# Decode attention over a long cache: one ring of aligned load slots on one queue, and V sums of 512 columns

## The chip, the cores and the metric

The kernel runs on one core of a Trainium2 chip. The metric is the device time of one execution in microseconds; a kernel's time is the median of its runs.

## The reference

One decode step of a transformer block for a batch of B = 2 with one new token each. All tensors are f32.

```python
xn = layernorm(x)                                  # x: (2, 1, 512)
q = (xn @ wq) as 32 heads of 128                   # wq: (512, 4096)
scores = q . k * 128 ** -0.5                       # k_cache: (2, 8, 32768, 128)
p = softmax(scores)                                # 4 query heads share one K and V head
o = p @ v                                          # v_cache: (2, 8, 32768, 128)
s = o @ wo                                         # wo: (4096, 512)
g = silu((relu(xn @ W_gate) * (xn @ W_up)) @ W_down)   # F = 1792
return x + s * g
```

The two caches are 268 MB each and every element is used once. The weights add 28 MB.

## The kernel before, in words

The caches are read in tiles of 4096 positions: 128 partitions x 32 rows x 128 floats, 2 MiB each, 16 KB a partition (NC = 4 pieces of NJ = 8 rows of DH = 128). There are 16 groups, one for each pair of batch and K/V head; a group has NU = 8 tiles of K and 8 of V. K tile and V tile t of the whole run are called k_t and v_t, t from 0 to 127.

One pass of the main loop, step s, works on K tile s and, OFF = 9 steps later, on V tile s - 9:

- k_transposes (L279): DVE transposes K tile s in two halves of 2048 columns (L284) into kts, of which there are two buffers.
- scores (L288): PE multiplies them with the queries, 16 matmuls of 256 columns in four column groups (L295). DVE takes the result out of PSUM, with the maximum of each row (L305).
- maximum (L309), once a group: PE and DVE bring the row maxima together and spread the negative maximum (nb, L329).
- weights (L332): ACT makes exponentials with their sums (L335), PE permutes them (pt, L339), DVE transposes them (pts, L343).
- values (L345): PE sums V over the positions of the tile. The four query heads of a group are the stationary operand, 128 x 4, and the moving operand is 128 x 128: 32 matmuls a tile (L351). They add up in one PSUM tile o_ps; row j goes to the column group j % 4.
- at a group's end: sums (L361) makes the reciprocal of the sum of the exponentials, take_o (L369) evicts o_ps, finish_group (L373) adds up the column groups with four small matmuls (L379) against the constant sel, and, every second group, multiplies with a tile of wo (L394) and adds to yacc, or, at the very end, forms the result (res).

Ahead of the loop stand the layer norm, the query projection (project_q, L184: 32 matmuls of 512 columns with the four tiles of wq, then copies and transposes) and, inside the first steps, the MLP (mlp_gu, mlp_down) with two tiles each of W_gate, W_up and W_down.

Loads. K tiles and wq share a pool of three 16 KB buffers (kpool), V tiles and the MLP weights another of three (vpool); wo has two buffers of its own. The function load (L116) gives the DMAs in turn to the queues of SP and ACT. The dictionary `ahead` says after which step of the loop a load is written: K tile t after step t - 2, V tile t after step t + 7. The very last V tile comes in three pieces (half, quarter, quarter).

The program is written in that order, but a scheduler then orders each engine's instructions, the DMA issues on SP and ACT among them; each engine runs its own list strictly in order. A DMA issue waits, on the engine that issues it, for the last reader of the buffer that it fills. Eight semaphores serve the DMAs in turn, so a DMA also waits until the one that last had its semaphore has landed.

Of the kernel before, what the change touches and what calls it, by code (L numbers as in the profile page):

```python
# [17 lines left out]
NBLK = NC * NJ  # L18
TK = P * NBLK
LAG = 1  # L20


@with_exitstack
def kernel(
# [37 lines left out]

    ident = const.tile([P, P], F32, name="ident")
    make_identity(nc, ident)
    sel = const.tile([P, REP], F32, name="sel")
    nc.vector.tensor_reduce(
        sel, ident.rearrange("p (g r) -> p r g", g=4)[:, :REP, :], axis=AX.X, op=ALU.add
    )
    same = const.tile([P, Q, REP], F32, name="same")
    nc.vector.tensor_reduce(  # L70
        same[:, 0, :],
# [41 lines left out]
    queues = [nc.sync, nc.scalar]  # L113
    issued = [0]

    def load(dst, src):  # L116
        queues[issued[0] % 2].dma_start(dst, src)
        issued[0] += 1

    def group(g):  # L120
        return g % B, g // B
# [10 lines left out]
            c += n  # L132

    def load_k(t):
        KT[t] = kpool.tile([P, NC, NJ, DH], F32, tag="k", name=f"k_{t}")
        load_tile(KT[t], kc, t, (NC,))

    def load_v(t):
        VT[t] = vpool.tile([P, NC, NJ, DH], F32, tag="v", name=f"v_{t}")
        load_tile(VT[t], vc, t, (NC,) if t < NG * NU - 1 else (2, 1, 1))  # L140

    def load_wo(hk):
        WO[hk] = work.tile([P, 2, 2, D], F32, tag="wo", name=f"wo_{hk}", bufs=2)
# [8 lines left out]
    wqt = {}  # L152

    def load_wq(k):
        wqt[k] = kpool.tile([P, 2, QW], F32, tag="k", name=f"wq_{k}")
# [6 lines left out]
    xc = const.tile([32, D], F32, name="xc")  # L162
    sq = const.tile([32, D], F32, name="sq")
# [20 lines left out]
    def project_q():  # L184
        pq = [ps_m.tile([P, 512], F32, tag="m", name=f"pq_{half}") for half in range(2)]
        for k in range(NKC):
            for half in range(2):
                for c in range(4):
                    nc.tensor.matmul(  # L189
                        pq[half][32 * c : 32 * c + 32, :],  # L190
                        xnt[:, k, :],
                        wqt[k][:, half, c * 512 : (c + 1) * 512],
                        start=(k == 0),
                        stop=(k == NKC - 1),
                    )
        for half in range(2):
            qs = work.tile([P, 512], F32, tag="row", name=f"qs_{half}")
            nc.vector.tensor_copy(qs, pq[half])
            for h in range(REP):
                rep = work.tile([P, 4, 4, Q], F32, tag="qrep", name=f"qrep_{half}_{h}")  # L200
# [16 lines left out]
    mlp = {}  # L217

    def load_gu(which, half):
        t = vpool.tile([P, 2, F], F32, tag="v", name=f"w{which}_{half}")  # L220
        w = wg if which == "g" else wu
        load(
            t.rearrange("p k f -> p (k f)"),
# [30 lines left out]
        mlp["ht"] = ht  # L254

    def load_d(half):
        t = vpool.tile([P, FH, D], F32, tag="v", name=f"wd_{half}")
# [87 lines left out]
    def values(t):  # L345
        g, u = divmod(t, NU)
        v, w = VT.pop(t), PT.pop(t)
        for c in range(NC):
            for j in range(NJ):
                a = j % 4  # L350
                nc.tensor.matmul(  # L351
                    o_ps[Q * a : Q * a + REP, :],
                    w[:, j, c * REP : (c + 1) * REP],
                    v[:, c, j, :],
                    start=(u == 0 and c == 0 and j < 4),
                    stop=(u == NU - 1 and c == NC - 1 and j >= 4),
                )

    OS, RL = {}, {}

# [6 lines left out]
        nc.vector.reciprocal(RL[g], pr[:, :1])  # L367

    def take_o(g):  # L369
        OS[g] = work.tile([P, P], F32, tag="os", name=f"os_{g}")  # L370
        nc.vector.tensor_scalar(OS[g], o_ps, RL.pop(g), None, op0=ALU.mult)  # L371

    def finish_group(g):  # L373
        b, hk = group(g)
        pr = ps_m.tile([P, 512], F32, tag="m", name=f"po_{g}")
        o2 = OS.pop(g).rearrange("p (q i) -> p i q", i=2)
        for i in range(2):
            for r in range(2):
                nc.tensor.matmul(  # L379
                    pr[64 * r : 64 * r + 64, i * REP : (i + 1) * REP],  # L380
                    o2[:, i, :],
                    sel,
                    start=True,
                    stop=True,
                )
# [31 lines left out]
        nc.vector.tensor_add(base, base, xy)  # L417

    for t in range(NK):
        at(ahead, t - 2, load_k, t)  # L420
        at(ahead, t + OFF - 2, load_v, t)
    for i in range(2):
        at(ahead, i - 2, load_gu, "g", i)
        at(ahead, i, load_gu, "u", i)
        at(ahead, i + 2, load_d, i)
# [8 lines left out]
    for s in sorted(k for k in ahead if k < 0):  # L434
        for f, a in ahead[s]:
            f(*a)
    project_q()

    for s in range(NK + OFF):
        v = s - OFF  # L440
# [52 lines left out]
```

## Time and profile before

| | |
|---|---|
| time, median of 3 runs | 1352.66 us (1352.29 to 1358.3) |
| the profiled execution: its own time / its span | 1354.88 us / 1352.5 us |
| PE busy (matmuls) | 856.8 us, 63% of the span, 13288 matmul instructions |
| DVE busy | 721.4 us, 53% |
| ACT busy | 73.5 us, 5% |
| read from HBM | 564.67 MB, 418 GB/s over the span |
| shares of the two load queues (q1, q10) | 49.8% and 49.0% of the 16 DMA engines' time |
| granted TensorE clock, mean | 0.804 |

How to read it. The span is the time from the first to the last instruction of the profiled execution; its own time is as the runs are timed, with what lies around the span. A row of a group of instructions reads: line, engine, operation, output<-inputs, partitions x elements, count | busy us, mean ns of one | idle time of the engine just before them and what ended it. A matmul in f32 is two instructions on PE, each with a weight load (PEld). In a row of waits stand who waited, for whom, us in total, how often, and the longest. A row of the timeline begins with the start and the length in us and merges neighbours of a kind. SPq and ACTq are the instruction queues of SP and ACT, from which DMAs are issued. GB/s is what all DMA engines moved, instruction fetches included.

### The profile page before, as it was taken

Reading aid. Unit: us, or ns where it says so; the run is one execution under the profiler, and the core shown is the slowest. Engines: PE = TensorE matmul, PEld = TensorE weight load, DVE = VectorE, ACT = ScalarE, POOL = GpSimd, SP = SyncE. Lnnn points to the kernel's source line nnn. Section 1 sums busy time; section 2 is a strip of 40 time slices with the busy share of each in tenths; the row PEclk is TensorE's granted clock in tenths of the full one; section 3 lists DMA queues with packets and bytes.
Section 4 is the critical chain, followed back from the end, with each engine's and each line's share of the span. In section 5 each row is a group of like instructions: output and inputs, shape, how many; then the busy total and the mean of one; then the engine's idle time right before and its main releaser. Section 6 shows DMA issues by size and latency. Waiting matters only on the chain.

```text
span 1352.5 us, 28835 instructions
## 1 busy us (share of the span) xinstructions
PE 856.8 (63%) x13288; PEld 502.2 (37%) x13288; DVE 721.4 (53%) x973; ACT 73.5 (5%) x261; POOL 1.3 (0%) x7
## 2 busy tenths in 40 slices
PE   2466667575765766557576656657666676665685
PEld 0123334334342433334333333433433343343454
DVE  2587655365554655454654655536555464635630
ACT  0002000000000100000000100000000010000010
POOL 0000000000000000000000000000000000000000
PEclk9678878778687878888878787878888788787887
DMA  9999999999999999999999999999999999999997
GB/s 398 428 378 414 421 430 429 429 404 429 430 429 430 427 430 429 429 430 429 429 430 430 418 428 430 428 431 415 427 430 429 429 406 430 430 429 407 390 393 292
DMA packets 40951, 566.52 MB, mean 419 GB/s; under 512 B 4462, under 2 KB 4478, under 8 KB 6784
## 3 DMA queue, kind: packets, MB, share of 16 engines
q1 hardware_dynamic: 20264, 284.70, 49.8%
q10 hardware_dynamic: 20536, 279.99, 49.0%
q8 instruction: 104, 1.70, 0.4%
q14 instruction: 15, 0.12, 0.0%
q0 software_dynamic: 32, 0.00, 0.0%
HBM read 564.67 MB, written 0.00 MB: 418 GB/s over the span
## 4 chain that ended last, share of the span: by engine, by line
issue 100%; POOLq 0%; POOL 0%
POOLq L488 0%; POOL ident masks.py:199 0%; POOL ident masks.py:197 0%; POOLq masks.py:199 0%; POOLq L475 0%
## 5 line engine op out<-in xcount | busy, mean ns | idle before, releaser
L284 DVE STREAM_TRANSPOSE kts<-k 128x2048 f32<-128x2048 f32 x256 | 585.2, 2295 | 337.5 <-DMA k<-in_A_k_cache_dram 337.4
L295 PE MATMUL s<-kts,qt 128*32 128x256 f32 x4096 | 418.3, 460 | 205.4 <-DVE kts L284 191.7
L351 PE MATMUL o_ps<-v,pts 128*4 128x128 f32 x8192 | 352.3, 327 | 243.5 <-DMA v<-in_A_v_cache_dram 218.5
L351 PEld LDWEIGHTS o_ps<-v,pts 128*4 128x4 f32 x8192 | 249.0, 100 | 347.6 <-issue 109.4
L295 PEld LDWEIGHTS s<-kts,qt 128*32 128x32 f32 x4096 | 178.5, 130 | 352.6 <-issue 188.9
L335 ACT ACTIVATE sc<-sc,nb 128x256 f32<-128x256 f32 x128 | 63.9, 499 | 1139.9 <-DVE nb L329 612.2
L305 DVE TENSOR_SCALAR_CACHE_REDUCE sc<-s 128x256 f32<-128x256 f32 x128 | 51.5, 402 | 137.0 <-PE s L295 136.6
L343 DVE STREAM_TRANSPOSE pts<-pt 128x256 f32<-128x256 f32 x128 | 55.1, 435 | 76.7 <-PE pt L339 67.5
L339 PE MATMUL pt<-sc,perm 128*128 128x256 f32 x256 | 95.6, 473 | 0.2 <-DVE l L363 0.2
L339 PEld LDWEIGHTS pt<-sc,perm 128*128 128x128 f32 x256 | 45.4, 213 | 52.5 <-issue 44.1
L335 ACT ACTIVATION_READ_ACCUMULATOR sc<-sc,nb 128x1 f32 x128 | 23.9, 187 | 0.0
L189 PE MATMUL pq<-wq,xnt 128*32 128x512 f32 x64 | 12.1, 908 | 9.4 <-DMA wq<-in_A_wq_dram 9.0
L211 DVE COPY qt<-pqt 32x16 f32<-32x16 f32 x64 | 8.6, 177 | 14.1 <-PE pqt L206 13.7
L394 PE MATMUL py<-wo,ot 128*32 128x128 f32 x256 | 15.8, 403 | 0.4 <-DVE ot L389 0.4
L371 DVE TENSOR_SCALAR os<-o_ps,rl 128x128 f32<-128x128 f32 x16 | 5.4, 338 | 19.0 <-PE o_ps L351 19.0
L233 PE MATMUL ps_u<-wu,xnp 128*32 128x448 f32 x32 | 6.5, 669 | 13.2 <-DMA wu<-in_B_W_up_dram 13.2
L394 PEld LDWEIGHTS py<-wo,ot 128*32 128x32 f32 x256 | 11.9, 162 | 4.4 <-issue 3.0
L389 DVE COPY ot<-po 64x4 f32<-64x4 f32 x32 | 5.1, 161 | 13.4 <-PE po L379 13.1
L329 DVE COPY nb<-pr 128x1 f32<-128x1 f32 x16 | 2.4, 148 | 18.1 <-PE pr L325 18.1
L177 PE MATMUL px<-ident,xc 32*128 32x32 f32 x4 | 0.9, 287 | 16.6 <-DVE xc L171 16.6
L305 DVE DVE_READ_ACCUMULATOR sc<-s 128x1 f32 x128 | 10.6, 83 | 0.0
L325 PEld LDWEIGHTS pr<-negone,mrow 1*128 1x128 f32 x32 | 6.5, 253 | 10.6 <-DVE os L371 7.3
(70 smaller groups left out, 111.1 us busy)
## 6 DMA issues: line engine op xcount, KB each, us to landing
k<-in_A_k_cache_dram SPq DMA_DIRECT2D x70, 2048.0 KB, 21.7
v<-in_A_v_cache_dram ACTq DMA_DIRECT2D x65, 2048.0 KB, 24.2
v<-in_A_v_cache_dram SPq DMA_DIRECT2D x62, 2048.0 KB, 22.1
k<-in_A_k_cache_dram ACTq DMA_DIRECT2D x58, 2048.0 KB, 23.9
wo<-in_A_wo_dram ACTq DMA_DIRECT2D x5, 1024.0 KB
wq<-in_A_wq_dram SPq DMA_DIRECT2D x2, 2048.0 KB, 12.7
wq<-in_A_wq_dram ACTq DMA_DIRECT2D x2, 2048.0 KB, 15.6
wg<-in_B_W_gate_dram ACTq DMA_DIRECT2D x2, 1792.0 KB, 12.5
```

Source lines behind the costliest of these rows:

```text
L189: nc.tensor.matmul(pq[half][32 * c : 32 * c + 32, :], xnt[:, k, :], wqt[k][:, half, c * 512 : (c + 1) * 512], start=(k == 0), stop=(k == N ...
L211: nc.vector.tensor_copy(qt[part, b, half * 4 : half * 4 + 4, :, kb * REP + h], src[:, :, :, b],)
L233: nc.tensor.matmul(ps[32 * c : 32 * c + 32, :FC], xnp[:, k, :], mlp[which, k][:, c * FC : (c + 1) * FC], start=(k == 0), stop=(k == NKC - 1),)
L284: nc.vector.transpose(KTS[t][:, i * half : (i + 1) * half], src[:, i * half : (i + 1) * half])
L295: nc.tensor.matmul(ps[Q * c : Q * c + Q, :], qt[:, b, hk, e, :], mov[:, e, c], start=(e == 0), stop=(e == 3),)
L305: nc.vector.tensor_scalar(ST[t], ps, SCALE, None, op0=ALU.mult, op1=ALU.max, accum_out=MX[g][:, u : u + 1])
L325: nc.tensor.matmul(pr[:, 256:257], mrow.rearrange("o c k h -> o (c k h)"), negone, start=True, stop=True)
L335: nc.scalar.activation(st, st, AF.Exp, bias=NBIAS[g], scale=1.0, accum_out=LS[g][:, u : u + 1])
L339: nc.tensor.matmul(ps, perm.rearrange("p k c h -> p (k c h)"), st, start=True, stop=True)
L343: nc.vector.transpose(PT[t].rearrange("p j m -> p (j m)"), ps)
L351: nc.tensor.matmul(o_ps[Q * a : Q * a + REP, :], w[:, j, c * REP : (c + 1) * REP], v[:, c, j, :], start=(u == 0 and c == 0 and j < 4), sto ...
L394: nc.tensor.matmul(py[32 * c : 32 * c + 32, :P], ot[:, k // 2, k % 2, :], WO[hk][:, k // 2, k % 2, c * P : (c + 1) * P], start=(k == 0), s ...
```

## The change

Four things change.

1. One pool, ring, with SLOTS = 8 slots of 16 KB takes the place of kpool, vpool and wo's two buffers. It is the first pool to be laid out, and each slot starts at a multiple of 512 bytes. K, V, wq, the MLP weights and wo all go through it. To make room, xp, xc, sq and the query copies (qrep) share one K^T buffer under the name boot.
2. All loads are issued by SP. Only x (boot, xy) and one piece of the result go through ACT.
3. Loads are written one step earlier (DEPTH = 3), V before K within a step, and each wo tile right behind the last V tile that is loaded for its head.
4. values sums with 8 matmuls a tile instead of 32: the stationary operand has the weights of all four pieces (128 x 16) and the moving operand one row j of all four (512 columns). o_ps grows to 128 x 512, of which only the blocks that belong together are used. take_o evicts 512 columns, and finish_group picks the blocks with 16 small matmuls instead of 4, against four versions of sel.

```diff
+LAST = (2, 1, 1)
+SLOTS = 8
+DEPTH = 3
+ALIGN = 512
...
+    ring = ctx.enter_context(tc.tile_pool(name="ring", bufs=SLOTS))
     const = ctx.enter_context(tc.tile_pool(name="const", bufs=1))
-    kpool = ctx.enter_context(tc.tile_pool(name="kpool", bufs=3))
-    vpool = ctx.enter_context(tc.tile_pool(name="vpool", bufs=3))
...
-    xp = const.tile([32, D], F32, name="xp")
+    boot = ktpool.tile([P, NBLK * DH], F32, tag="kt", name="boot")
+    xp, xc, sq = (boot[:32, i * D : (i + 1) * D] for i in range(3))
+    reps = [boot[:, (3 + i) * 512 : (4 + i) * 512] for i in range(2)]
...
-    o_ps = ps_p.tile([P, P], F32, name="o_ps", bufs=1)
+    o_ps = ps_p.tile([P, NC, DH], F32, name="o_ps", bufs=1)
...
-        queues[issued[0] % 2].dma_start(dst, src)
-        issued[0] += 1
+        nc.sync.dma_start(dst, src)
...
-        KT[t] = kpool.tile([P, NC, NJ, DH], F32, tag="k", name=f"k_{t}")
+        KT[t] = ring.tile([P, NC, NJ, DH], F32, tag="r", align_bytes=ALIGN, name=f"k_{t}")
...
-        for c in range(NC):
+        c = 0
+        for n in (NC,) if t < NK - 1 else LAST:
             for j in range(NJ):
-                a = j % 4
+                a = Q * (j % 4)
                 nc.tensor.matmul(
-                    o_ps[Q * a : Q * a + REP, :],
-                    w[:, j, c * REP : (c + 1) * REP],
-                    v[:, c, j, :],
+                    o_ps[a : a + n * REP, :n, :],
+                    w[:, j, c * REP : (c + n) * REP],
+                    v[:, c : c + n, j, :],
...
+            c += n
...
-                nc.tensor.matmul(
-                    pr[64 * r : 64 * r + 64, i * REP : (i + 1) * REP],
-                    o2[:, i, :],
-                    sel,
-                    start=True,
-                    stop=True,
-                )
+                for c in range(NC):
+                    nc.tensor.matmul(
+                        pr[64 * r : 64 * r + 64, i * REP : (i + 1) * REP],
+                        o2[:, c, i, :],
+                        sel[:, c, :],
+                        start=(c == 0),
+                        stop=(c == NC - 1),
+                    )
...
-        at(ahead, t - 2, load_k, t)
-        at(ahead, t + OFF - 2, load_v, t)
+        at(ahead, t - DEPTH, load_k, t)
+        at(ahead, t + OFF - DEPTH, load_v, t)
...
-        at(ahead, (hk * B + B - 1) * NU + OFF + NU // 2 - 1, load_wo, hk)
+        at(ahead, (hk * B + B) * NU - 1 + OFF - DEPTH, load_wo, hk)
```

How the change moves instructions shows at three places. The names carry numbers: k_28 is K tile 28, sc_19 the scores of K tile 19, pt_8 and pts_8 the permuted and the transposed weights of tile 8, s_16 the score sums of K tile 16; the last number is that of the buffer.

The first place is the issue of loads in the third group. ACT before, whose list holds every second load, here the K tiles:

```order
L117 DMA k_28_1908<-in_A_k_cache_dram 128x4096
L335 ACTIVATE sc_19_1376,ls_2_1709<-sc_19_1376,nb_2_1707 128x256
L117 DMA k_29_1971<-in_A_k_cache_dram 128x4096
L335 ACTIVATE sc_20_1439,ls_2_1709<-sc_20_1439,nb_2_1707 128x256
L117 DMA k_30_2034<-in_A_k_cache_dram 128x4096
L335 ACTIVATE sc_21_1504,ls_2_1709<-sc_21_1504,nb_2_1707 128x256
```

SP in the changed kernel, which has them all:

```order
L123 DMA v_14_1196<-in_A_v_cache_dram 128x4096
L123 DMA k_23_1198<-in_A_k_cache_dram 128x4096
L123 DMA v_15_1235<-in_A_v_cache_dram 128x4096
L123 DMA k_24_1237<-in_A_k_cache_dram 128x4096
L123 DMA wo_0_1239<-in_A_wo_dram 128x2x1024
L123 DMA v_16_1276<-in_A_v_cache_dram 128x4096
L123 DMA k_25_1278<-in_A_k_cache_dram 128x4096
```

On ACT the K loads stood between exponentials of the group at hand; on SP there are loads alone, V and K in turn, in the order in which they are used.

The second place is a group's boundary on PE, from the last V tile of the first group on (pr_1 belongs to the maximum of the second group, pl_0 to the sum of the first, po to finish_group). Before:

```order
L351 MATMUL o_ps_123<-v_7_1070,pts_7_1099 4x128 x15
L295 MATMUL s_16_1140<-kts_16_1137,qt_114 32x256 x14
L313 MATMUL pr_1_1162<-ident_82,m_1_1160 1x128
L365 MATMUL pl_0_1181<-l_0_1179,same_89 128x1
L295 MATMUL s_17_1233<-kts_17_1230,qt_114 32x256 x5
L325 MATMUL pr_1_1162<-negone_101,mrow_99 128x1
L295 MATMUL s_17_1233<-kts_17_1230,qt_114 32x256 x4
L379 MATMUL po_0_1219<-sel_87,os_0_1217 64x4 x4
```

And in the changed kernel:

```order
L316 MATMUL pr_1_988<-ident_79,m_1_986 1x128
L371 MATMUL pl_0_1007<-l_0_1005,same_89 128x1
L355 MATMUL o_ps_123<-v_7_881,pts_7_949 16x512 x4
L328 MATMUL pr_1_988<-negone_101,mrow_99 128x1
L355 MATMUL o_ps_123<-v_7_881,pts_7_949 16x512 x3
L342 MATMUL pt_8_1001<-sc_8_665,perm_96 128x256
L386 MATMUL po_0_1021<-sel_84,os_0_1019 64x4 x16
L342 MATMUL pt_9_1067<-sc_9_710,perm_96 128x256
L342 MATMUL pt_10_1106<-sc_10_749,perm_96 128x256
L342 MATMUL pt_11_1145<-sc_11_788,perm_96 128x256
L342 MATMUL pt_12_1184<-sc_12_827,perm_96 128x256
L298 MATMUL s_16_966<-kts_16_963,qt_114 32x256 x16
```

Before, the scores of K tiles 16 and 17 stood ahead of and between the steps of the maximum; now the scores of K tile 16 come behind the whole maximum and five tiles of weights. DVE's list has its two transposes of K tile 16 behind pts_10 in the same way.

The third place is the end of the loads. SP before (ACT had v_120, v_122, v_124, two pieces of v_127 and, ahead of these, wo_7):

```order
L117 DMA v_119_8686<-in_A_v_cache_dram 128x4096
L117 DMA v_121_8815<-in_A_v_cache_dram 128x4096
L117 DMA v_123_8893<-in_A_v_cache_dram 128x4096
L117 DMA v_125_8971<-in_A_v_cache_dram 128x4096
L117 DMA v_126_9012<-in_A_v_cache_dram 128x4096
L117 DMA v_127_9051<-in_A_v_cache_dram 128x1024
```

SP in the changed kernel:

```order
L123 DMA v_125_6152<-in_A_v_cache_dram 128x4096
L123 DMA v_126_6167<-in_A_v_cache_dram 128x4096
L123 DMA v_127_6182<-in_A_v_cache_dram 128x2048
L123 DMA v_127_6182<-in_A_v_cache_dram 128x1024 x2
L123 DMA wo_7_6186<-in_A_wo_dram 128x2x1024
```

The last tile of wo, before issued ahead of V tile 120, is now the last load of all.

More of the change, by code (lines that the diff above doesn't have):

```diff
@@ L64 @@
     make_identity(nc, ident)
-    sel = const.tile([P, REP], F32, name="sel")
-    nc.vector.tensor_reduce(
-        sel, ident.rearrange("p (g r) -> p r g", g=4)[:, :REP, :], axis=AX.X, op=ALU.add
-    )
+    sel = const.tile([P, NC, REP], F32, name="sel")
+    for c in range(NC):
+        nc.vector.tensor_reduce(
+            sel[:, c, :],
+            ident.rearrange("p (g r) -> p r g", g=4)[:, c * REP : (c + 1) * REP, :],
+            axis=AX.X,
+            op=ALU.add,
+        )
     same = const.tile([P, Q, REP], F32, name="same")
@@ L134, in load_k @@
     def load_k(t):
-        KT[t] = kpool.tile([P, NC, NJ, DH], F32, tag="k", name=f"k_{t}")
+        KT[t] = ring.tile([P, NC, NJ, DH], F32, tag="r", align_bytes=ALIGN, name=f"k_{t}")
         load_tile(KT[t], kc, t, (NC,))
     def load_v(t):
-        VT[t] = vpool.tile([P, NC, NJ, DH], F32, tag="v", name=f"v_{t}")
-        load_tile(VT[t], vc, t, (NC,) if t < NG * NU - 1 else (2, 1, 1))
+        VT[t] = ring.tile([P, NC, NJ, DH], F32, tag="r", align_bytes=ALIGN, name=f"v_{t}")
+        load_tile(VT[t], vc, t, (NC,) if t < NG * NU - 1 else LAST)
     def load_wo(hk):
-        WO[hk] = work.tile([P, 2, 2, D], F32, tag="wo", name=f"wo_{hk}", bufs=2)
+        WO[hk] = ring.tile([P, 2, 2, D], F32, tag="r", align_bytes=ALIGN, name=f"wo_{hk}")
         r = REP * DH
@@ L154, in load_wq @@
     def load_wq(k):
-        wqt[k] = kpool.tile([P, 2, QW], F32, tag="k", name=f"wq_{k}")
+        wqt[k] = ring.tile([P, 2, QW], F32, tag="r", align_bytes=ALIGN, name=f"wq_{k}")
         load(wqt[k].rearrange("p h n -> p (h n)"), wq[k * P : (k + 1) * P, :])
@@ L161 @@
     st = const.tile([32, 8], F32, name="st")
-    xc = const.tile([32, D], F32, name="xc")
-    sq = const.tile([32, D], F32, name="sq")
     nc.vector.reduce_sum(st[:, 0:1], xp, axis=AX.X)
@@ L199, in project_q @@
             for h in range(REP):
-                rep = work.tile([P, 4, 4, Q], F32, tag="qrep", name=f"qrep_{half}_{h}")
+                rep = reps[h % 2].rearrange("p (e k l) -> p e k l", e=4, k=4)
                 qh = qs[:, h * DH : (h + 1) * DH].rearrange("p (e l) -> p e l", l=Q)
@@ L219, in load_gu @@
     def load_gu(which, half):
-        t = vpool.tile([P, 2, F], F32, tag="v", name=f"w{which}_{half}")
+        t = ring.tile([P, 2, F], F32, tag="r", align_bytes=ALIGN, name=f"w{which}_{half}")
         w = wg if which == "g" else wu
@@ L256, in load_d @@
     def load_d(half):
-        t = vpool.tile([P, FH, D], F32, tag="v", name=f"wd_{half}")
+        t = ring.tile([P, FH, D], F32, tag="r", align_bytes=ALIGN, name=f"wd_{half}")
         load(
@@ L347, in values @@
         v, w = VT.pop(t), PT.pop(t)
-        for c in range(NC):
+        c = 0
+        for n in (NC,) if t < NK - 1 else LAST:
             for j in range(NJ):
-                a = j % 4
+                a = Q * (j % 4)
                 nc.tensor.matmul(
-                    o_ps[Q * a : Q * a + REP, :],
-                    w[:, j, c * REP : (c + 1) * REP],
-                    v[:, c, j, :],
-                    start=(u == 0 and c == 0 and j < 4),
-                    stop=(u == NU - 1 and c == NC - 1 and j >= 4),
+                    o_ps[a : a + n * REP, :n, :],
+                    w[:, j, c * REP : (c + n) * REP],
+                    v[:, c : c + n, j, :],
+                    start=(u == 0 and j < 4),
+                    stop=(u == NU - 1 and c + n == NC and j >= NJ - 4),
+                    skip_group_check=True,
                 )
+            c += n
     OS, RL = {}, {}
@@ L369, in take_o @@
     def take_o(g):
-        OS[g] = work.tile([P, P], F32, tag="os", name=f"os_{g}")
+        OS[g] = work.tile([P, NC, DH], F32, tag="os", name=f"os_{g}")
         nc.vector.tensor_scalar(OS[g], o_ps, RL.pop(g), None, op0=ALU.mult)
@@ L375, in finish_group @@
         pr = ps_m.tile([P, 512], F32, tag="m", name=f"po_{g}")
-        o2 = OS.pop(g).rearrange("p (q i) -> p i q", i=2)
+        o2 = OS.pop(g).rearrange("p c (q i) -> p c i q", i=2)
         for i in range(2):
             for r in range(2):
-                nc.tensor.matmul(
-                    pr[64 * r : 64 * r + 64, i * REP : (i + 1) * REP],
-                    o2[:, i, :],
-                    sel,
-                    start=True,
-                    stop=True,
-                )
+                for c in range(NC):
+                    nc.tensor.matmul(
+                        pr[64 * r : 64 * r + 64, i * REP : (i + 1) * REP],
+                        o2[:, c, i, :],
+                        sel[:, c, :],
+                        start=(c == 0),
+                        stop=(c == NC - 1),
+                    )
         o3 = pr[:, : 2 * REP].rearrange("p (i c r) -> p c i r", i=2, r=2)
@@ L432 @@
     at(extra, NK + OFF - 2, make_base)
-    for s in sorted(k for k in ahead if k < 0):
+    for f, a in ahead[-DEPTH] + ahead[1 - DEPTH]:
+        f(*a)
+    project_q()
+    for s in range(2 - DEPTH, 0):
         for f, a in ahead[s]:
             f(*a)
-    project_q()
     for s in range(NK + OFF):
```

8 lines of the change are left out of this document (3 added, 5 removed).

## The prediction

> **What bounds the kernel now.** I read the page first, for the loads:
>
> ```profile
> span 1352.5 us, 28835 instructions
> DMA  9999999999999999999999999999999999999997
> GB/s 398 428 378 414 421 430 429 429 404 429 430 429 430 427 430 429 429 430 429 429 430 430 418 428 430 428 431 415 427 430 429 429 406 430 430 429 407 390 393 292
> DMA packets 40951, 566.52 MB, mean 419 GB/s; under 512 B 4462, under 2 KB 4478, under 8 KB 6784
> q8 instruction: 104, 1.70, 0.4%
> ```
>
> Most slices stand at 427 to 431 GB/s; about ten fall to 292 to 421. The DMA digit is 9 in nearly all of them, so it does not tell good slices from bad; GB/s does. Next I asked for stretches, cut where the rate changes; the last three columns are the granted clock, the DMA share and GB/s:
>
> ```profile
> core 0: us, PE busy (x) PEld busy (x) DVE busy (x) ACT busy (x) POOL busy (x), PEclk, DMA share, GB/s
> 0.00:50.00 50.00, 21.76 (x134) 6.62 (x135) 19.25 (x64) 1.58 (x2) 0.70 (x6) 0.86 0.97 408
> 50.00:120.00 70.00, 36.87 (x437) 17.74 (x435) 48.91 (x102) 2.84 (x3) 0.00 (x0) 0.78 0.98 396
> 120.00:250.00 130.00, 86.35 (x1359) 51.70 (x1363) 76.57 (x93) 8.09 (x32) 0.00 (x0) 0.82 1.01 427
> 250.00:310.00 60.00, 38.41 (x577) 21.37 (x568) 34.11 (x39) 3.88 (x14) 0.00 (x0) 0.75 0.99 414
> 310.00:760.00 450.00, 288.35 (x4540) 170.77 (x4540) 240.94 (x289) 22.57 (x82) 0.00 (x0) 0.79 1.01 429
> 760.00:1200.00 440.00, 285.37 (x4513) 170.25 (x4513) 241.15 (x293) 26.03 (x96) 0.00 (x0) 0.82 1.00 426
> 1200.00:1265.00 65.00, 42.89 (x625) 25.78 (x629) 34.45 (x47) 3.28 (x12) 0.00 (x0) 0.76 0.96 398
> 1265.00:1305.00 40.00, 26.13 (x486) 16.42 (x479) 20.40 (x30) 1.09 (x4) 0.00 (x0) 0.90 1.01 428
> 1305.00:1346.00 41.00, 28.76 (x594) 20.32 (x593) 4.35 (x14) 4.15 (x16) 0.00 (x0) 0.77 0.89 354
> 1346.00:1352.50 6.50, 1.88 (x56) 1.23 (x44) 1.26 (x5) 0.00 (x0) 0.65 (x1) 0.93 0.00 1
> ```
>
> For 450 us on end (310 to 760) the loads run at 429 GB/s while PE is busy 64% and DVE 54%. I take 429 as the rate of a fed DMA. All bytes at that rate are 566.52 MB / 429 GB/s = 1320.6 us, so 31.9 us of the span are holes. By stretch, each us x (1 - GB/s / 429): 2.4 at the start, then 5.4, 0.6, 2.1, 0, 3.1, 4.7, 0.1 and 7.2, and 6.5 after the last load; 32.1 together. The kernel is bound by its loads, and the middle holes are 23.2 us.
>
> Why are there holes? The waits of SP's own queue:
>
> ```profile
> SPq L117 <- PE o_ps L351: 370.4, 64, 29.4
> SPq L117 <- DMA v<-in_A_v_cache_dram: 260.2, 48, 17.4
> SPq L117 <- DMA k<-in_A_k_cache_dram: 224.1, 56, 11.2
> SPq L117 <- DVE kts L284: 192.1, 30, 24.3
> ```
>
> A load waits until PE or DVE has freed one of only three buffers of its kind, and then often longer, for an earlier DMA. The two kinds do not share buffers: at the end only V is left and three of the six 16 KB buffers serve it, and that is the worst stretch (354). In between, ACT's half of the loads stands among its exponentials, which wait for a group's maximum.
>
> **The change part by part.** *The ring.* Eight slots serve loads strictly in order of use, so load n+8 waits for the user of load n, and for nothing else that is late. A 2 MiB load takes 2.097 MB / 429 = 4.9 us. When load n lands, seven others are issued or issuable, 34 us of DMA work. The queue runs dry only if a slot is still held about 34 us after its landing, less the time that an idle queue needs to begin, bounded above by a 1 KB transfer's 1.6 us from issue to landing; so 32 us decide. What holds a slot:
>
> ```profile
> out_dram<-res POOLq DMA_DIRECT2D x1, 1.0 KB, 1.6
> L284 DVE STREAM_TRANSPOSE kts<-k 128x2048 f32<-128x2048 f32 x256 | 585.2, 2295 | 337.5 <-DMA k<-in_A_k_cache_dram 337.4
> L295 PE MATMUL s<-kts,qt 128*32 128x256 f32 x4096 | 418.3, 460 | 205.4 <-DVE kts L284 191.7
> L351 PE MATMUL o_ps<-v,pts 128*4 128x128 f32 x8192 | 352.3, 327 | 243.5 <-DMA v<-in_A_v_cache_dram 218.5
> 1291.83 2.30 DVE L284 STREAM_TRANSPOSE kts<-k 128x2048 f32<-128x2048 f32 x1
> 1308.63 0.45 DVE L343 STREAM_TRANSPOSE pts<-pt 128x256 f32<-128x256 f32 x1 [2.38 <-PE pt L339]
> ```
>
> A K tile is held for two transposes, 2 x 2.295 = 4.6 us; a V tile for 352.3 / 128 = 2.8 us. The exception is a group boundary, where the new order puts the next group's first scores (PE) and transposes (DVE) behind the whole chain maximum, exponential, first weights. That chain, from the last K tiles (1291.83) to the first weights (1309.08), lasts 17.3 us, a wait of PE for a V tile included. Add the tile's own 4.6 and it is 21.9, below 32. Behind the waiting SP instruction stand all further loads; none is late as long as this holds. DVE catches up afterwards: 54% busy. So I take nothing for it (bounds 0, and 16 boundaries of a few us: below).
>
> At the start the first eight loads (four of wq, two of K, two of the gate: 6 x 2.097 + 2 x 1.835 = 16.25 MB) keep the DMA busy until about 2.4 + 37.9 = 40 us, and the ninth needs only the projection from the first wq, which before began at 18 us. The thirteenth (about 59 us) needs K tile 0, transposed before by 45.2 us:
>
> ```profile
> 18.00 6.49 PE L189 MATMUL pq<-wq,xnt 128*32 128x512 f32 x32 [0.39 <-DVE xnt L181]
> 42.85 2.30 DVE L284 STREAM_TRANSPOSE kts<-k 128x2048 f32<-128x2048 f32 x1
> ```
>
> The initial 2.4 us stay. The boot buffer, shared by the query work and a K^T tile, delays only K tile 1, whose slot the fifteenth load asks for near 68 us (28.05 MB before it). x now leaves ACT's queue ahead of the weights, so the layer norm comes earlier, hidden under wq. All 23.2 us of middle holes go.
>
> *One queue.* Does one queue reach 429? In 286 to 292 us the loads came from ACT's queue (q10) alone:
>
> ```profile
> DMA packets 175, 2.57 MB, mean 429 GB/s; under 512 B 18, under 2 KB 18, under 8 KB 18
> q10 hardware_dynamic: 174, 2.57, 100.1%
> ```
>
> 2.57 MB is more than one tile, so a change of load inside one queue is in it: cost 0. The Trainium skill's "DMA: Bandwidth & Descriptors", section "Anatomy of one DMA", gives each DMA a fixed 2.0 us beside its bytes; if one queue exposed that at each of 276 loads, an estimate from that page would be 550 us more. The stretch just quoted shows none of it.
>
> *Alignment.* The six big buffers before begin at multiples of 512 as built; only the wo tiles did not. Taken as 0.
>
> *Sums over V.* 32 matmuls a tile become 8 of 512 columns. The same shape in the query projection, 16 instructions (a matmul counts as two here):
>
> ```profile
> 26.01 1.92 PE L189 MATMUL pq<-wq,xnt 128*32 128x512 f32 x16 [1.52 <-DMA wq<-in_A_wq_dram]
> 35.42 3.64 PE L189 MATMUL pq<-wq,xnt 128*32 128x512 f32 x16 [7.49 <-DMA wq<-in_A_wq_dram]
> ```
>
> So 1.9 to 3.6 us a tile instead of 2.8: between 0.9 saved and 0.8 lost, all beside loads (9.8 us a step, of which PE is busy 64%). Time from this alone: 0; without that cover the 0.8 would cost 128 x 0.8 = 102 us. The wider eviction and finish of a group hide likewise. It does shorten the program: 8192 - 2048 matmuls, each with its weight load, leave 12288 fewer instructions; the fourfold sums in a group's finish add 16 x 24 x 2 = 768; 17.3 thousand remain. Instruction fetches (1.70 MB on the same engines) fall by 40%, 0.68 MB, 1.6 us.
>
> *The tail.*
>
> ```profile
> 1344.24 2.15 PE L351 MATMUL o_ps<-v,pts 128*4 128x128 f32 x64 [0.57 <-DMA v<-in_A_v_cache_dram]
> 1346.87 0.41 PE L379 MATMUL po<-sel,os 128*64 128x4 f32 x8 [0.49 <-DVE os L371]
> 1347.72 1.08 PE L394 MATMUL py<-wo,ot 128*32 128x128 f32 x32 [0.44 <-DVE ot L389]
> L198 DVE COPY qs<-pq 128x512 f32<-128x512 f32 x2 | 1.2, 664 | 0.0
> ```
>
> Before, V's last matmuls end at 1346.39; the last quarter of 64 takes about 0.6, so the loads end near 1345.8, and py starts 1.9 later. Now wo's last tile (1.05 MB, 2.4 us) lands behind V. After V: 0.6 of matmuls, the old 1.3 to py, 0.3 more for evicting 512 columns (664 ns for that shape) and about 1.0 for 32 small matmuls instead of 8: 3.2, or 0.8 after wo. So 1.1 us are gained (bounds 2 gained, 1 lost). On the clock: the slow row above (3.64) came after a wait of 7.49. The Trainium skill's "TensorE: Matmul & The Clock Gate", section "Part 1: The HAM clock gate", says the array falls to half clock after an idle window of about 3.4 us; PE idles more between V tiles now, and by that rule the tail's 2 us of PE work could double, making the sum 1 to 2 us longer. The pair of rows agrees with it.
>
> *Sum.* 1352.5 - 23.2 - 1.6 - 1.1 = 1326.6 of span. That execution took 1354.88 in all, 2.4 outside its span; the median of the runs, 1352.66, is 0.2 above the span, so a median of **1327 us**, 1.9% faster.
>
> **The rivals.**
> (a) *Part of the holes is not waiting.* The shares fall less than the rates: against 1.01, the deficits are 0.03 x 70, 0.02 x 60, 0.01 x 440, 0.05 x 65 and 0.12 x 41 = 15.9 us of the 23.2. The other 7.3 are packets that run long; if these have another cause than refilling an empty queue they stay: 1334. Against: they are long only near idle stretches.
> (b) *The holes move to the boundaries,* about as large as before: 1346 to 1359. For: the new order at a boundary. Against: the 21.9 us.
> (c) *Slower: one late slot stops everything.* A single in-order queue has no second one to go on with. It decides when a slot is held over 32 us: if the boundary chain doubled, 2 x 17.3 + 4.6 = 39.2, 7.2 us would be lost 16 times, 115 us: about 1442; at 35 us it is 3 x 16, about 1375. Nothing in the trace is that long.
> (d) *Slower: every load exposes its start and end* on one queue; with 1.6 us (the 1 KB row) x 276 = 440 us: 1767. The 429 row speaks against it.
> (e) *Only alignment or a deeper queue lifts the rate itself* over 429: at 432, 0.7% or 9 us less, 1318. Against: buffers already aligned, 429 to 431 wherever fed.
>
> **How the numbers follow.** The forecast has 0.80; its own range is 1321 to 1333 (rate 428 to 430, 3 us each way, and the tail's bounds). (a) 0.09, (b) 0.03, (c) 0.04, (d) 0.01, (e) 0.03. The range 1319 to 1340 holds the forecast, (a) and the edge of (e). What a measurement can tell from no change is 0.5%, 6.8 us: faster means under 1345.9. Forecast, (a) and (e) all lie there, less a little of (a) that I shift to the middle: faster 0.90, same 0.05, slower 0.05.
>
> **What would show it.** Right: GB/s at 427 to 431 in every slice but the first and last, all bytes on one queue, SP waiting for PE and DVE alone in the middle, DVE still waiting for K; instructions near 17.3 thousand; wo landing last, py within a us of it. Wrong: slices under 425 at a period of one group, some 80 us (b, c); a rate under 425 with the queue never empty (d); PE's V row over 5 us a tile.

## The result, and the profile after

The changed kernel takes 1333.68 us (median of 4 runs, 1332.56 to 1335.89), the kernel before, run beside it, 1354.36 us (1352.29 to 1358.3). The ratio is 0.9846, 95% interval 0.9832 to 0.986: 20.7 us faster. The forecast was 1327 us, 25.7 us under the 1352.66 us that it started from. So the time is 6.7 us longer than the sum said, and the gain 5 us smaller. The direction, the range and most of the mechanism held.

The page of the changed kernel, for the loads (GB/s in 40 equal slices, then the queues):

```profile
span 1334.0 us, 17338 instructions
GB/s 397 429 431 429 431 430 430 429 431 431 429 430 431 430 430 430 429 430 432 430 430 422 428 430 431 429 416 429 429 430 430 415 430 429 431 431 414 430 430 283
DMA packets 40907, 565.79 MB, mean 424 GB/s; under 512 B 4462, under 2 KB 4478, under 8 KB 6784
q1 hardware_dynamic: 40776, 564.68, 99.4%
q8 instruction: 60, 0.98, 0.3%
```

The early dips of before are gone: one queue, q1, moves 429 to 431 GB/s slice after slice. Four slices in the second half fall to 414 to 422, at every second group's boundary; x (1 - GB/s / 430) x 33.35 us they make 4.1 us. The last slice, 283, is much like before's, 292. What SP waits for (us in total, times, longest):

```profile
SPq L123 <- PE o_ps L355: 568.6, 120, 10.4
SPq L123 <- DVE kts L287: 448.3, 112, 10.1
SPq L123 <- PE py L401: 60.1, 7, 8.6
```

But for some 9 us on loads of wq and K, SP no longer waits for an earlier DMA, only for the work that frees slots, and there never longer than 10.4 us. The groups of instructions show something that was not forecast:

```profile
L287 DVE STREAM_TRANSPOSE kts<-k 128x2048 f32<-128x2048 f32 x256 | 572.7, 2275 | 0.0
L298 PE MATMUL s<-kts,qt 128*32 128x256 f32 x4096 | 466.7, 522 | 388.9 <-DVE kts L287 373.7 <-DVE l L369 9.4 <-DVE qt L214 3.2
L308 DVE TENSOR_SCALAR_CACHE_REDUCE sc<-s 128x256 f32<-128x256 f32 x128 | 54.3, 425 | 375.5 <-PE s L298 375.5
L355 PE MATMUL o_ps<-v,pts 128*16 128x512 f32 (+2 forms) x2080 | 360.2, 675 | 0.0
```

DVE, 55% busy, does not wait for K at all: it transposes, waits for PE's scores (375.5 us in all), transposes again, and PE waits for the transposes (373.7 us). A step is a trip DVE, PE, DVE in series, nearly as long as its loads, so landed tiles pile up in the ring. The V sums, in the last row, gain nothing on PE: 360.2 us over 128 tiles are 2.8 us a tile, as before. In this execution the last V sums come in one lump and late:

```profile
1317.72 8.80 PE L355 MATMUL o_ps<-v,pts 128*16 128x512 f32 x112
1327.40 1.46 PE L386 MATMUL po<-sel,os 128*64 128x4 f32 x32 [0.87 <-DVE os L377]
1329.29 1.08 PE L401 MATMUL py<-wo,ot 128*32 128x128 f32 x32 [0.43 <-DVE ot L396]
```

So the first theory was: the lag costs the 4 us of holes and some 3 us of a late end, and that is the miss. The experiments contradict it.

### The profile page after: what moved, and what is told of

It reads as the page before. It is cut to its first block, busy times and chain, and to the rows that moved or that the text cites. A ratio compares the mean times of both kernels' runs of the same rounds, so it can differ in the third digit from the quotient of the medians.

```text
span 1334.0 us, 17338 instructions
## 1 busy us (share of the span) xinstructions
PE 881.1 (66%) x7560; PEld 345.6 (26%) x7560; DVE 736.5 (55%) x976; ACT 69.1 (5%) x261; POOL 1.3 (0%) x7
## 4 chain that ended last, share of the span: by engine, by line
issue 100%; POOLq 0%; POOL 0%
POOLq L497 0%; POOL ident masks.py:199 0%; POOL ident masks.py:197 0%; POOLq masks.py:199 0%; POOLq L484 0%
## 5 line engine op out<-in xcount | busy, mean ns | idle before, releaser
L298 PE MATMUL s<-kts,qt 128*32 128x256 f32 x4096 | 466.7, 522 | 388.9 <-DVE kts L287 373.7
L287 DVE STREAM_TRANSPOSE kts<-k 128x2048 f32<-128x2048 f32 x256 | 572.7, 2275 | 0.0
L355 PE MATMUL o_ps<-v,pts 128*16 128x512 f32 (+2 forms) x2080 | 360.2, 675 | 0.0
L308 DVE TENSOR_SCALAR_CACHE_REDUCE sc<-s 128x256 f32<-128x256 f32 x128 | 54.3, 425 | 375.5 <-PE s L298 375.5
L355 PEld LDWEIGHTS o_ps<-v,pts 128*16 128x16 f32 (+2 forms) x2080 | 96.2, 116 | 141.6 <-issue 130.1
L342 PE MATMUL pt<-sc,perm 128*128 128x256 f32 x256 | 85.3, 439 | 33.4 <-DVE pts L346 32.2
L342 PEld LDWEIGHTS pt<-sc,perm 128*128 128x128 f32 x256 | 42.5, 198 | 99.7 <-issue 73.0
L386 PE MATMUL po<-sel,os 128*64 128x4 f32 x512 | 23.4, 204 | 3.9 <-DVE os L377 3.9
L386 PEld LDWEIGHTS po<-sel,os 128*64 128x64 f32 x512 | 22.0, 138 | 10.2 <-DVE os L377 10.2
L377 DVE TENSOR_SCALAR os<-o_ps,rl 128x512 f32<-128x512 f32 x16 | 12.0, 750 | 17.3 <-PE o_ps L355 17.3
L401 PE MATMUL py<-wo,ot 128*32 128x128 f32 x256 | 19.2, 403 | 0.4 <-DVE ot L396 0.4
L308 DVE DVE_READ_ACCUMULATOR sc<-s 128x1 f32 x128 | 10.7, 83 | 0.0
```

What stands on the lines that cost most here:

```text
L287: nc.vector.transpose(KTS[t][:, i * half : (i + 1) * half], src[:, i * half : (i + 1) * half])
L298: nc.tensor.matmul(ps[Q * c : Q * c + Q, :], qt[:, b, hk, e, :], mov[:, e, c], start=(e == 0), stop=(e == 3),)
L308: nc.vector.tensor_scalar(ST[t], ps, SCALE, None, op0=ALU.mult, op1=ALU.max, accum_out=MX[g][:, u : u + 1])
L342: nc.tensor.matmul(ps, perm.rearrange("p k c h -> p (k c h)"), st, start=True, stop=True)
L355: nc.tensor.matmul(o_ps[a : a + n * REP, :n, :], w[:, j, c * REP : (c + n) * REP], v[:, c : c + n, j, :], start=(u == 0 and j < 4), stop=( ...
L386: nc.tensor.matmul(pr[64 * r : 64 * r + 64, i * REP : (i + 1) * REP], o2[:, c, i, :], sel[:, c, :], start=(c == 0), stop=(c == NC - 1),)
```

## The experiments

Each time stands beside runs of the kernel before on the same chip (medians 1354.5 to 1355.0); ratios are to those.

### Transposes ahead of the scores' eviction

```diff
-        if s < NK:
-            k_transposes(s)
-            scores(s)
+        if s == 0:
+            k_transposes(0)
+        if s + 1 < NK:
+            k_transposes(s + 1)
+        if s < NK:
+            with tc.issue_after(TR[min(s + 1, NK - 1)].ins):
+                scores(s)
```

TR holds the second transpose of each tile; issue_after keeps the eviction on DVE behind it. Below, this kernel is called the one with the transposes ahead.

> The transposes of K tile s+1 are put ahead of the eviction of the scores of tile s on DVE, so that DVE transposes while PE multiplies; nothing else changes. Theory 1 (a step of the changed kernel is a serial trip DVE, PE, DVE about as long as its loads, so the ring slowly fills with landed tiles): the waits of DVE for PE's scores (375 us) fall below 100 us, DVE waits for K again, the four holes (4.4 us) go and the V sums end about 3 us earlier: 1325 to 1328 us instead of 1333.7. Theory 2 (the wo tiles, which hold ring slots until py, make the holes): the four holes stay where they are, at every second group's boundary, 1332 to 1334. Theory 3 (the wider eviction and the 16 small matmuls at a group's end make the boundary too long): the holes stay too, 1332 to 1334.

Measured: 1332.57 us (1332.06 to 1332.91), ratio 0.9838 (0.9825 to 0.9851). GB/s, the instruction fetches, and two groups of DVE:

```profile
GB/s 396 431 430 430 430 431 430 430 429 432 429 431 430 430 430 431 428 431 431 431 429 431 430 429 430 431 430 429 430 431 430 430 431 429 429 430 430 431 430 274
q8 instruction: 59, 0.97, 0.3%
```

```profile
L288 DVE STREAM_TRANSPOSE kts<-k 128x2048 f32<-128x2048 f32 x256 | 573.4, 2278 | 88.7 <-DMA k<-in_A_k_cache_dram 88.5
L309 DVE TENSOR_SCALAR_CACHE_REDUCE sc<-s 128x256 f32<-128x256 f32 x128 | 49.3, 385 | 3.0 <-PE s L299 3.0
```

Every sign of theory 1 came true: the wait for scores falls from 375.5 to 3.0 us, DVE waits for K again, no slice between the first and the last is under 428. Only the time did not follow: 1 us instead of 6 to 9. Where it goes shows at the end. Stretches of the last 26 us (start and end, length, the granted clock, the busy share of the 16 DMA engines, GB/s):

```profile
1304.00:1312.00 8.00, 1.00 1.02 430
1312.00:1316.00 4.00, 1.00 0.69 287
1316.00:1320.00 4.00, 0.71 0.55 230
1320.00:1324.00 4.00, 0.87 0.38 157
1324.00:1328.00 4.00, 0.99 0.01 3
```

All loads had been issued by 1298 us, and nothing waits for a slot; yet from about 1312 us the share falls to 0.55, that is to 9 of 16 engines, and those need 12 us more. The engines do not end together: each works through its own part of every tile, and here, where the queue is never empty, some are 12 us behind at the end. The missing shares, 0.31 x 4 + 0.45 x 4 + 0.62 x 4, are 5.5 us of all 16. The kernel before shows none of this:

```profile
1342.00:1343.00 1.00, 0.50 0.97 369
1343.00:1344.00 1.00, 0.50 0.80 320
1344.00:1345.00 1.00, 0.63 0.23 94
1345.00:1346.00 1.00, 1.00 0.02 8
```

There the engines end within some 2 us of each other. The likely reason is that its waits for earlier DMAs let the slower ones catch up; no run tests that by itself.

### wo outside the ring

```diff
-        WO[hk] = ring.tile([P, 2, 2, D], F32, tag="r", align_bytes=ALIGN, name=f"wo_{hk}")
+        WO[hk] = work.tile([P, 2, 2, D], F32, tag="wo", name=f"wo_{hk}", bufs=1)
```

> The changed kernel with wo's tiles in one buffer of their own, outside the ring; the ring then holds K, V and MLP tiles alone. Theory 1 (serial step): the lag of the work behind the loads is the same, only the slot that a wo tile held comes free: of the 7.4 us at most 2 us are won, 1332 to 1334. Theory 2 (wo tiles in the ring): the holes near 728, 885, 1047 and 1207 us go, 1328 to 1330, the late V sums at the end stay. Theory 3 (wider finish): no change, 1333 to 1334.

Measured: 1332.94 us (1332.01 to 1335.68), ratio 0.984 (0.9827 to 0.9854). GB/s:

```profile
GB/s 396 430 431 431 430 429 431 430 430 430 429 432 430 428 430 431 430 430 430 431 430 430 429 430 431 430 429 430 430 430 421 427 430 430 430 418 429 429 431 255
```

Two dips (421 and 418) are left of four, with no difference in time that can be told. So the slot that a wo tile holds has a part in the dips, but theory 2's 1328 to 1330 us fall.

### The ring alone, and the sums alone

The ring alone is the changed kernel with values, take_o, finish_group, sel and o_ps of before; the sums alone are the kernel before with those of the changed kernel.

> The ring, the one queue and the earlier loads, but the sums over V as before: 32 matmuls of 128 columns a tile, the 128-column eviction and four small matmuls at a group's end. Theory 1: the sums take 2.75 us a tile instead of 2.8, so the step is as long as in the changed kernel; 12 thousand instructions more are fetched (1.6 us), the end is 1 us shorter: 1332 to 1336. Theory 3 (wider finish makes the holes): the holes go, 1328 to 1331. A rival to the forecast as a whole (the 512-column sums bring a good part of the gain): 1340 to 1348.

> The kernel before with the 512-column sums, the wider eviction and the 16 small matmuls alone; buffers and queues as before. The forecast and theory 1: nothing but the instruction fetches, 0 to 2 us less than before: 1351 to 1355. The rival (the sums bring a good part of the gain): 1340 to 1346. Theory 3 (the wider finish costs at every boundary): slower than before by 16 times 0.3 to 1 us, 1357 to 1368.

Measured: the ring alone 1338.45 us (1338.32 to 1339.06), ratio 0.9883 (0.9869 to 0.9896); the sums alone 1360.42 us (1358.99 to 1362.91), ratio 1.0046 (1.0029 to 1.0063). On the first all three forecasts missed, on the second all but theory 3's. The ring alone has no dips in the middle, and its V row nearly the same PE time (351.5 us, 360.2 in the changed kernel); its fetches, that row, and the end:

```profile
q8 instruction: 104, 1.70, 0.5%
L350 PE MATMUL o_ps<-v,pts 128*4 128x128 f32 x8192 | 351.5, 296 | 10.4 <-DMA v<-in_A_v_cache_dram 9.6
```

```profile
1312.00:1316.00 4.00, 1.00 0.73 311
1316.00:1320.00 4.00, 0.93 0.56 231
1320.00:1324.00 4.00, 0.65 0.49 208
1324.00:1328.00 4.00, 1.00 0.50 209
1328.00:1332.00 4.00, 1.00 0.39 154
```

Again about 7 of 16 engines are through at 1312 to 1316 us, as in the run above. The others, 8 or 9 of them, go on to some 1331 us instead of 1324. What differs on the DMA engines is the number of instruction fetches, 104 instead of 59.

So theory 4, which the next run tests: about half of the engines also serve the instruction fetches and fall behind by them, and the slowest engines set the end.

### Sums of 256 columns

The kernel with the transposes ahead, and in values:

```diff
-        for n in (NC,) if t < NK - 1 else LAST:
+        for n in (2, 2) if t < NK - 1 else LAST:
```

This changes a part of the computation: in the first tile of a group the second pass over the rows starts the sums anew in all four column groups, so that what the first pass summed, the tile's first two pieces, is left out. The work is the same.

> The kernel of the run with the transposes put ahead (1332.57 us), with 16 matmuls of 256 columns a tile for the sums over V instead of 8 of 512: the same columns in all, 4 thousand instructions more, about 76 instruction fetches instead of 60. Theory 4 (only about half of the 16 DMA engines serve the instruction fetches, each of 16 KB holds its engine up some 1.35 us, and the loads of one queue are not shared out anew, so the slowest engines set the end): the fast engines run out of loads at 1312 to 1315 us as before, the slow ones 16 / 8 x 1.35 = 2.7 us later than the 1324.3 of that run: 1334.5 to 1336. Rival (fetches are spread over all engines like any other bytes, 0.26 MB at 429 GB/s): 0.6 us more, 1332.5 to 1333.5.

Measured: 1334.83 us (1334.78 to 1335.27), ratio 0.9863 (0.9849 to 0.9878). Fetches, the V row and the end:

```profile
q8 instruction: 75, 1.23, 0.3%
```

```profile
L356 PE MATMUL o_ps<-v,pts 128*8 128x256 f32 (+1 forms) x4112 | 331.0, 417 | 9.0 <-DMA v<-in_A_v_cache_dram 8.9
```

```profile
1312.00:1316.00 4.00, 1.00 0.67 284
1316.00:1320.00 4.00, 0.53 0.57 241
1320.00:1324.00 4.00, 0.61 0.50 207
1324.00:1328.00 4.00, 1.00 0.25 99
```

The time and the end come out as theory 4 said, and the rival's 0.6 us does not: again about 7 engines are done by 1316 us, the rest at some 1327 us. With 59, 75 and 104 fetches the loads end near 1324, 1327 and 1331 us, 12, 15 and 19 us behind the first engines. That is about 0.2 us of lag for each fetch, where the forecast took 0.04 (16 KB at 429 GB/s). In the kernel's time it is a little less: 2.3 us for 16 fetches more, 5.9 us for 45.

Are the slow engines those that serve the fetches? The trace does not name the engine of a packet, but it has the start and the length of each one. On a fed engine a 16 KB packet takes 611 ns and the next one starts 607 ns after it, so the packets can be strung into 16 chains, one for each engine. In the kernel with the transposes ahead, from 190 us on, the 16 KB fetches fall on eight chains, always in the same turn, six or seven on each. A ninth chain has seven of the smaller fetches of 8 KB (queue q14). These nine chains run out of loads at 1320.0 to 1324.3 us. The other seven, with no 16 KB fetch and at most three small ones, do so at 1312.6 to 1315.1 us. In the run with the uneven tile, below, the chains up to that tile show it again: eight in the same turn, and seven without.

One fetch holds its engine up by 1.43 us in the mean: 0.93 us for itself, and 1.11 instead of 0.61 us for the load packet behind it (theory 4 had taken 1.35). For 60 fetches on eight engines that is 7.5 x 1.43 = 10.7 us, most of the 12; for 75 it is 13.4, for 104 it is 18.6. So theory 4 is shown, with eight engines as its "about half".

### Alignment

The sums alone had one more clue:

```profile
GB/s 399 423 379 410 420 427 425 427 425 428 425 427 428 413 426 426 425 425 426 428 426 426 411 423 426 427 425 425 426 427 424 429 414 427 426 425 422 423 380 250
```

Its fed slices stand at 425 to 428, not 429 to 431. The larger sel, laid out ahead of the buffers, had moved the six big ones 32 bytes off. Two kernels test this, the changed one with its ring moved, and the sums alone with sel padded to 544 bytes:

```diff
-ALIGN = 512
+ALIGN = 32
...
+    pad = ctx.enter_context(tc.tile_pool(name="pad", bufs=1))
+    eps_t = pad.tile([P, 8], F32, name="eps_t")[:32, :1]
     ring = ctx.enter_context(tc.tile_pool(name="ring", bufs=SLOTS))
```

```diff
-    sel = const.tile([P, NC, REP], F32, name="sel")
+    sel = const.tile([P, 136], F32, name="sel")[:, : NC * REP].rearrange("p (c r) -> p c r", c=NC)
```

> The changed kernel with its ring begun 32 bytes off a multiple of 64 (a small constant is laid out ahead of it), all else alike. Theory 5 (the sums alone were slower than before because their larger constant had moved the six big buffers 32 bytes off, and packets into such buffers run longer): slices of 425 to 427 GB/s where the changed kernel has 429 to 431, 1339 to 1347 us. Rival (the sums alone were slower for another reason, and 64-byte alignment costs nothing): 1332 to 1336, slices as in the changed kernel.

> The kernel before with the 512-column sums, the wider eviction and the 16 small matmuls, as in the run of the sums alone (1360.42), but with the larger constant padded so that the six big buffers stay at multiples of 512. Theory 5 (alignment): slices back at 428 to 430 GB/s and 6 to 12 us less than that run, 1347 to 1354. Rival (the sums or their finish themselves cost 5 us in the kernel before): 1358 to 1362.

Measured: the moved ring 1341.61 us (1341.52 to 1342.28), ratio 0.9914 (0.9899 to 0.9928); the sums alone, aligned, 1351.14 us (1343.57 to 1354.09), ratio 0.9968 (0.9949 to 0.9988). The GB/s rows of the two:

```profile
GB/s 398 425 428 426 429 427 429 424 428 427 426 429 425 428 427 427 428 427 426 428 428 427 427 427 428 428 425 428 427 427 428 426 427 427 428 427 425 427 428 269
```

```profile
GB/s 398 426 376 412 426 432 428 431 431 430 431 428 432 412 429 431 429 430 430 431 430 430 420 428 432 429 430 428 432 428 432 430 403 428 431 430 430 430 343 228
```

Thirty-two bytes cost some 8 us in the ring and some 9 in the kernel before. The packets show it directly: from 190 to 1240 us the median 16 KB load takes 611 ns in the changed kernel and in the sums alone, aligned, but 613 and 614 ns in the two with moved buffers, where at least a tenth of the packets take 620 ns and more. Only this one offset was tried. Theory 3 falls too: the sums with their wider finish, aligned, make the kernel before 3.5 us faster, with 60 fetches instead of 104; what the finish costs within that was not separated.

### Two queues

```diff
+    queues = [nc.sync, nc.scalar]
+    issued = [0]
...
-        nc.sync.dma_start(dst, src)
+        queues[issued[0] % 2].dma_start(dst, src)
+        issued[0] += 1
```

> The changed kernel with its loads issued by SP and ACT in turn instead of by SP alone; ring, alignment, order of loads and sums as in the changed kernel. If one queue or two is all one (the forecast): 1332 to 1336. Rival (ACT's exponentials then stand behind loads that wait for a slot, and half of the loads behind exponentials that wait for a group's maximum): holes come back at the boundaries, 1340 to 1355.

Measured: 1333.13 us (1332.81 to 1334.79), ratio 0.9853 (0.9836 to 0.9871). That SP issues all loads is worth nothing by itself.

### An uneven tile

The kernel with the transposes ahead, and one V tile loaded in two parts:

```diff
+UNEVEN = (112,)
...
+        if src is vc and t in UNEVEN:
+            load(flat[:119], rows[:119])
+            load(flat[119:], rows[119:])
+            return
```

> The kernel with the transposes put ahead (1332.57 us), whose seven first engines were out of loads at 1312.5 to 1314.5 us while the last one worked until 1324.3; V tile 112 alone is loaded by two DMAs, of 119 partitions and of 9, and so not evenly by all 16 engines. The Trainium skill's page DMA: Bandwidth & Descriptors, section Why a DMA increments its semaphore by 16 and not by 1, says that a DMA from SP runs on the largest number of engines up to 16 that divides its partitions, and on the lowest-numbered ones; by that page the 119 go to engines 0 to 6, 17 packets each, and the 9 to engines 0 to 8, one each. In packets of 611 ns that is 18 instead of 8 for each of seven engines (6.1 us more) and none for seven others (4.9 us less). Theory 4a (the slow engines, which serve the instruction fetches, are among those that are spared): all end near 1319 us, 1326 to 1329. Theory 4b (the slow engines are those that get more): the end moves out by 6 us, 1337 to 1340. Rival (the engines' ends have nothing to do with what each has to move, or the loads are shared out as they come free): 1332 to 1333.

Measured: 1356.36 us (1354.91 to 1358.45), ratio 1.0013 (1.0004 to 1.0022). No theory foresaw this. The stretches around that tile:

```profile
1150.00:1190.00 40.00, 0.83 1.01 431
1190.00:1200.00 10.00, 0.83 1.01 399
1200.00:1250.00 50.00, 0.70 1.01 277
1250.00:1300.00 50.00, 0.75 1.01 430
```

For 50 us the rate is 277 GB/s while the engines are busy throughout, so packets run long. The stretch explains 50 x (1 - 277 / 430) = 17.8 us of the 24 that this run is slower than the one without the uneven tile; the rest lies at the end, where the DMA share falls over a longer time (from 0.96 at 1320 to 1330 us to 0.10 at 1345 to 1350 us). The experiment does not tell 4a from 4b; whether work can be moved from the slow engines to the fast ones stays open.

### Lag and depth, side by side

The changed kernel, the one with the transposes ahead, and the latter with SLOTS = 6, on one chip.

> The changed kernel once more, on the same chip as the next two, so that its time and theirs can be compared. Theory 4 (the slowest DMA engines set the end; the four holes in the changed kernel are mostly time in which engines that are ahead anyway stand idle): 1332.5 to 1336, of which the lag of the work behind the loads is worth 1 to 3 us. Theory 1 as first priced (lag and holes are the whole miss): 5 us or more above the next kernel.

> The kernel with the transposes put ahead, once more, beside the changed kernel on one chip. Theory 4: 1331.5 to 1333, 1 to 3 us less than the changed kernel, and less scattered. Theory 1 as first priced: 1325 to 1328.

> The kernel with the transposes put ahead and a ring of six slots instead of eight. With eight it had 2.4 to 4 tiles outstanding at its lowest, so with six 0.4 to 2, less what the fast engines are ahead (up to 2 tiles late in the run): the fast engines run dry now and then. Theory 4 (only the slowest engines set the end): slices of 415 to 428 GB/s late in the run, but the loads end where they did, 1324 to 1327, and the time stays at 1332 to 1336. Rival (a hole costs what it is long, as the forecast counted all holes): 1337 to 1345, by as much as the slices fall short of 430.

Measured: 1332.68 us (1332.63 to 1336.44), 1332.38 us (1331.87 to 1333.14) and 1332.13 us (1331.95 to 1332.58); ratios 0.9842 (0.9824 to 0.9859), 0.9833 (0.9819 to 0.9847), 0.9831 (0.9817 to 0.9845). GB/s of the first and the last:

```profile
GB/s 397 429 431 431 430 430 430 429 432 429 430 431 429 429 431 431 428 431 431 431 429 430 429 431 430 431 430 426 430 431 431 412 429 431 430 428 416 428 431 301
```

```profile
GB/s 397 430 429 431 431 429 430 431 429 432 430 431 429 429 431 431 428 432 430 430 431 429 431 430 430 430 419 430 431 429 429 421 431 429 429 431 431 431 428 297
```

Slices of 412, 416, 419 and 421 cost nothing: what a dip loses in the middle the last slice has more (301 and 297 instead of 274). That fits engines that are ahead anyway standing idle in them. The medians of the three cannot be told apart; the lag shows only in a scatter upwards, to 1336.44. So no version here beats the changed kernel by more than a measurement can tell.

## Why the forecast was right, and where its sum failed

**Direction and mechanism.** Right: the kernel is bound by its loads, and the ring takes the long waits for buffers away. The ring alone gains 16.3 us (1354.79 to 1338.45), the sums within it about 5 more. But the 1333.68 us lie just above the forecast's own 1321 to 1333, in the part of the range that was there for rival (a).

**The step that failed** is the sum of bytes over a rate: "I take 429 as the rate of a fed DMA", hence "All 23.2 us of middle holes go". It treats 16 engines as one pipe whose holes are all lost time. They are 16 pipes with equal shares of the loads, of which nine carry something more. Once the queue is never empty, as in the kernel with the transposes ahead, the first engines are through at 1312 us, sooner than the forecast's 429 would have them, and the last at 1324 us, later than its end of loads (a span of 1326.6, less 6.5 - 1.1 behind the loads: 1321.2 us). So 3 us of what was counted as holes could not be won by filling the queue. That slow engines used them before to catch up fits the common end there, but was not tested. Ring and tail were put at 24.3 us, and the ring alone, with all its 104 fetches, brought 16.3.

**The fetches.** From the same cause the term "1.6 us" for 44 fetches fewer was too small: the kernels with 104 fetches and with 59 or 60 lie 5 to 6 us apart in the ring. So the 512-column sums, priced at nothing on PE (rightly: 351.5 and 360.2 us), are worth about a quarter of the gain, by the length of the program: a shorter one delays the eight engines less often.

**From span to time.** The forecast put the median 0.2 us above the span, by a first median of 1352.66 us. The runs beside the later kernels have medians of 1354.36 to 1355.02 us, and the profiled execution of the second series of the changed kernel takes 1332.68 us at a span of 1330.9: 1.8 us above. That is 1.6 us of the miss. The 2.4 us of the first profiled execution were at hand, and the forecast set them aside for a median and a span of two different executions. With the 3 us above it makes 4.6 of the 6.7 us; the rest goes by the late end and the scatter of single executions, which no run measures apart (the second series of the changed kernel has a median 1 us lower).

**Late work.** "DVE catches up afterwards: 54% busy. So I take nothing for it" was wrong as a statement and right as a price. A busy share of 55% left no slack, as the idle time lay inside a serial step; the sign "DVE still waiting for K" did not come. On one chip the difference is 0.3 us, within the scatter.

**The tail.** py was to start within a us of wo's landing. In the profiled execution V's sums were late by 3 us; prompt, as in the run with the transposes ahead, py starts at 1325.55 us, 1.2 us behind the last load (1324.3) and behind the chain os, po, ot:

```profile
1323.66 1.46 PE L387 MATMUL po<-sel,os 128*64 128x4 f32 x32 [0.88 <-DVE os L378]
1325.55 1.08 PE L402 MATMUL py<-wo,ot 128*32 128x128 f32 x32 [0.43 <-DVE ot L397]
```

The 1.46 us of po against 0.41 before are the 1.0 us more that the sum had. The slower clock that the tail's paragraph considered did not come: from 1324 to 1328 us the granted clock was 0.99 in this run and 1.00 in the changed kernel.

**One queue, alignment, the number of instructions.** Right. One queue or two is the same; six big buffers were aligned before, and aligned they stayed; 17338 instructions were forecast as 17.3 thousand. The 550 us that an estimate from the Trainium skill's "DMA: Bandwidth & Descriptors", section "Anatomy of one DMA", would have added appear in no run; that section's 2.0 us are fitted to DMAs issued from GpSimd, while all loads here are issued by SP or ACT.

**The rivals.** (a) gave 1334 us and 1333.7 came out, but that agreement is luck: its long packets went with the idle stretches, as some 430 in every middle slice of the kernel with the transposes ahead shows. (b) falls with the GB/s rows: the dips at the boundaries make 4.1 us, not some 23. (c) falls with SP's longest wait for a slot, 10.4 us, and with the equal time of six slots and eight. (d) and (e) fall with 429 to 431 GB/s, neither less nor more, wherever the queue is fed.

## What to carry to other kernels

When loads bound a kernel, look at the end of the loads, not only at the holes in the middle: if the DMA share falls in steps while nothing waits, the engines are out of step, and the slowest sets the time. Then a hole in the average rate may cost nothing, and every 16 KB of program that is fetched, some 280 instructions, costs 0.13 to 0.2 us here. A constant that grows ahead of the load buffers can cost more than the edit that needs it brings, so pin their alignment.

## What the runs showed of the hardware

- The 16 KB instruction fetches fall on eight of the 16 DMA engines in turn, and each holds its engine up by 1.43 us. So the engines of a queue that is never empty drift apart, 12 to 19 us by the end. The Trainium skill's "DMA: Bandwidth & Descriptors", section "Why a DMA increments its semaphore by 16 and not by 1", says that the engines of a DMA finish independently and that only the full count means that all has landed; the tails above agree (7 of 16 through 12 us ahead of the rest).
- A ring 32 bytes off a multiple of 512 loads at 424 to 429 GB/s instead of 429 to 431, 8 us here.
- One tile of 119 and 9 partitions instead of 128 costs 24 us, most of it in 50 us at 277 GB/s with all engines busy. Why its neighbours suffer too was not tried.
